# An order of their own for the first three halves of a clustered attention, with four stack copies on GpSimd and the loads re-ordered

## The chip, the core and the metric

One core of one Trainium2 chip runs the whole program in one launch: clustered attention, then two mixture-of-experts-like layers. The metric is the device time of an execution in microseconds (us). The kernel before takes 1053.87 us, the median of three runs (1053.55 to 1054.81). The engines are PE (TensorE: matmuls; its weight loads are shown apart as PEld), DVE (VectorE), ACT (ScalarE), POOL (GpSimd) and SP (SyncE, which here issues every DMA). Each engine works through its own list of instructions in the order in which the kernel wrote them, and waits at an instruction until what that one needs is there. All matmuls here have fp32 operands or fp32r (fp32 with the value rounded for TensorE's one-pass format).

## What is computed

The inputs are q, k, v of 2 batches x 8 heads x 768 rows x 64, and 16 centroids per head.

```python
q_assign = argmax(q_n @ c_n.T, -1)          # q_n, k_n, c_n: rows of unit length
k_assign = argmax(k_n @ c_n.T, -1)
scores = q @ k.T / 8
scores = where(q_assign[:, None] == k_assign[None, :], scores, -1e9)
x = softmax(scores) @ v                     # 1536 tokens x 512 after the heads are put side by side
g = elu(x @ w_in); x = g @ w_out            # 512 -> 2048 -> 512
p = probs / probs.sum(-1)                   # 4 experts, all of them used
out = sum_e p[:, e] * (relu(x @ w1[e]) @ w2[e])
```

## The kernel before

Attention goes through 8 pairs of heads (pair 0 is batch 0, heads 0 and 1). For each pair q and k are loaded, transposed by PE (tile `qkps`, line 199), and split into a high part that is exact in fp32r (`qh`, `kh`, ACT, line 201) and the rest (`ql`, `kl`, DVE, line 203). PE multiplies them with the centroids (`lps`, lines 239 and 240), ACT and DVE add the parts of that (`ltmp` line 243, `L` line 245), and the argmax over 16 centroids is a reduce, a subtract, a compare with a ramp (which breaks ties), a second reduce and an equality (lines 267 to 276: `mx`, `L`, `rk`, `mx`, `oh`). PE transposes the one-hot rows (`ohps`), and they become 16 more rows of the operands of the scores, so that the mask is part of the matmul: for the first pair in `first_onehot` (lines 304 and 306), later in `prep_onehot`.

The operands of one head's scores are four tiles, its *stacks*: QA (high q twice), KA (high k, low k), QB (one-hot rows, low q) and KB (one-hot rows, high k). The parts are 64 rows by 768, and `prep_stacks` (line 228) moves each of them from `qh`, `ql`, `kh`, `kl` with a DMA of 192 KB, six for a head. The next pair's `qh` and `kh` go to the same buffers, so they wait until those DMAs have read them.

The scores are taken in *units* of 128 query rows x 768 keys, numbered u0, u1, ... from the start (6 units to a head). Two units make a *half*, numbered w0, w1, ...; six halves make a pair. A half goes through these steps, and the letters are those of the table `AT` in the code: S scores (PE, lines 364 and 367, two buffers in PSUM), M the negated maximum of a row (DVE, line 373), E exponential and row sum (ACT, line 382), G and R the reciprocal of the sums of both units (lines 390, 394), P the scaling (POOL, line 400), T 12 transposes in three groups of four (PE, line 412, three buffers that they share with `qkps`, `lps` and `ohps`), C and L the split of a group into `ph` and `pl` (ACT line 425 and DVE line 433; for some groups ACT copies to `raw`, line 422, and POOL does both parts, lines 430 and 431), V 12 matmuls with v (PE, line 441), and X, Y, Z the sum of the two parts (ACT line 453, DVE line 461, POOL). Q are pieces of the next pairs' preparation, W pieces of the weights of the layers behind.

The order is a list: each step of each half has a time, `AT` plus 4.6 for every half plus a few shifts, and all are sorted by it and written out in that order, so each engine's list follows from it. What stands ahead of the list (the prologue) is written out by hand: loads, preparation of the first pair, 14 transposes of the identity that only keep PE at work (`warm`, line 508), the argmax of the first head. The second head's argmax, its one-hot rows and the next pair's q are put in ahead of three items of half w0.

The layers behind attention (lines 745 to 931) start when it ends, in a fixed order of their own.

## Time and profile before

| | us |
|---|---|
| median of three runs | 1053.87 |
| the profiled execution | 1049.63 |
| its span, from the first instruction to the last | 1047.9 |
| attention, about | 0 to 268 |
| PE busy, share of the span | 98% |
| DVE, ACT, POOL busy, share of the span | 70%, 50%, 37% |

The shares mix two stages: behind attention PE works almost alone, and in attention four engines are near their limit together. What the change does lies in the first 45 us, so the shares of that stretch are the ones to read. The first unit's scores start at 17.6 us, and the first exponential at 21.5 us. The page names 67.5 MB of DMA; the mean busy share of the DMA engines is 0.8 and 0.7 in the first two of its 40 slices.

### The profile page before, as it was taken

What the parts mean: (1) busy time and instruction counts of PE and PEld (TensorE: products, weight loads), DVE (VectorE), ACT (ScalarE), POOL (GpSimd) and SP (SyncE); (2) the same over time, 40 slices, a digit from 0 to 9 for tenths busy, and PEclk for the clock granted to TensorE, in tenths of its full rate; (3) what the DMA queues carried; (4) which work ended last, traced back from release to release, by engine and by line L of the source; (5) the groups of instructions that cost most, each with busy time, mean ns of one, the idle gap of its engine ahead of it and who ended that gap; (6) DMA issues with size and microseconds to landing.
All of it is one profiled execution on the core that took longest, in us unless ns stands there. A gap on an engine that the chain in (4) does not pass through costs nothing.

```text
span 1047.9 us, 16446 instructions
## 1 busy us (share of the span) xinstructions
PE 1029.1 (98%) x6253; PEld 918.4 (88%) x6253; DVE 735.4 (70%) x1248; ACT 524.2 (50%) x1081; POOL 392.8 (37%) x394
## 2 busy tenths in 40 slices
PE   8999999999999999999999999999999999999998
PEld 7989999989877888888888898999999898989897
DVE  6999989998689674326576765666666767666665
ACT  4989999988676563324442332233332333332331
POOL 2888888889578766344641000000000000000000
PEclk8999999999999999999999999999999999999999
DMA  8746664431323221010002101111101111001003
GB/s 184 186 109 155 144 145 104 111 92 33 114 96 122 81 96 66 1 41 0 1 1 81 41 1 41 41 41 41 35 7 41 41 42 41 17 25 41 1 1 121
DMA packets 61790, 67.53 MB, mean 64 GB/s; under 512 B 29008, under 2 KB 47440, under 8 KB 61712
## 3 DMA queue, kind: packets, MB, share of 16 engines
q1 hardware_dynamic: 61712, 66.49, 22.4%
q8 instruction: 49, 0.80, 0.3%
q14 instruction: 29, 0.24, 0.1%
HBM read 43.08 MB, written 3.15 MB: 44 GB/s over the span
## 4 chain that ended last, share of the span: by engine, by line
PE 84%; DVE 8%; ACT 4%; issue 2%; DMA 1%; SPq 1%; POOL 1%; DVEq 0%; ACTq 0%; POOLq 0%
PE a L915 35%; PE h L765 23%; PE h L745 10%; PE x L441 5%; PE tps L412 4%; PE s L364 2%; PE s L367 2%; DVE pl L433 2%; DVE nm L373 1%; PE lps L239 1%; PE lps L240 1%; DVE wa L710 1%; ACT ph L425 1%; PE qkps L199 1%; ACT e L382 1%
## 5 line engine op out<-in xcount | busy, mean ns | idle before, releaser
L765 PEld LDWEIGHTS h<-x,w1op 128*128 128x128 f32 x2016 | 257.4, 190 | 10.3 <-ACT r L776 1.2
L765 PE MATMUL h<-x,w1op 128*128 128x256 f32 x2016 | 261.2, 285 | 1.0 <-ACT r L776 1.0
L915 PE MATMUL a<-w2op,gh 128*128 128x512 f32 x768 | 238.4, 392 | 0.0
L915 PEld LDWEIGHTS a<-w2op,gh 128*128 128x128 f32 x768 | 138.0, 188 | 23.9
L924 DVE SCALAR_TENSOR_TENSOR acc<-a,prob,acc 128x512 f32<-128x512 f32 x180 | 129.7, 746 | 40.2 <-PE a L915 40.2
L915 PE MATMUL a<-w2op,gl 128*128 128x512 f32 x384 | 149.8, 390 | 0.0
L745 PE MATMUL h<-xT,wh 128*128 128x512 f32 x384 | 118.5, 390 | 0.6 <-DVE gg L754 0.5
L400 POOL TENSOR_SCALAR p<-e,sm 128x768 f32<-128x768 f32 x96 | 88.4, 927 | 40.2 <-DVE sm L394 29.0
L754 DVE SCALAR_TENSOR_TENSOR gg<-r,h 128x512 f32<-128x512 f32 x48 | 32.9, 685 | 96.5 <-ACT r L753 75.4
L373 DVE TENSOR_REDUCE nm<-s 128x1 f32<-128x768 f32 x96 | 90.9, 947 | 2.8 <-PE s L367 2.6
L382 ACT ACTIVATE e<-s,nm 128x768 f32<-128x768 f32 x96 | 86.6, 902 | 4.5 <-POOL p L400 2.8
L412 PE MATMUL tps<-ident,p 128*128 128x128 f32 x576 | 83.5, 277 | 2.9 <-DVE pl L433 2.7
L745 PEld LDWEIGHTS h<-xT,wh 128*128 128x128 f32 x384 | 71.9, 188 | 16.2 <-DVE gg L754 1.4
L776 ACT ACTIVATE r<-h 128x256 f32<-128x256 f32 x48 | 18.4, 384 | 134.8 <-PE h L765 134.8
L915 PEld LDWEIGHTS a<-w2op,gl 128*128 128x128 f32 x384 | 72.1, 188 | 15.6
L433 DVE TENSOR_TENSOR pl<-tps,ph 128x512 fp32r<-128x512 f32 x112 | 76.2, 683 | 6.6 <-ACT ph L425 5.2
L441 PE MATMUL x<-ph,v 128*128 128x256 f32 x288 | 76.6, 298 | 1.4 <-DVE xs L461 1.3
L752 ACT ACTIVATE r<-h 128x512 f32<-128x512 f32 x48 | 28.6, 595 | 97.7 <-PE h L745 96.9
L915 PE MATMUL a<-gh,wh 128*128 128x512 f32 x192 | 74.9, 390 | 1.0 <-ACT acc L931 0.9
L755 POOL TENSOR_SCALAR gh<-gg 128x512 fp32r<-128x512 f32 x48 | 41.0, 854 | 92.0 <-DVE gg L754 89.2
L915 PE MATMUL a<-gl,wh 128*128 128x512 f32 x192 | 74.8, 390 | 0.0
L915 PE MATMUL a<-gh,wl 128*128 128x512 f32 x192 | 74.7, 389 | 0.0
(152 smaller groups left out, 1942.1 us busy)
## 6 DMA issues: line engine op xcount, KB each, us to landing
st<-in_moe_w_dram SPq DMA_DIRECT2D x32, 512.0 KB, 4.3
st<-in_moe_w_in_dram SPq DMA_DIRECT2D x14, 512.0 KB, 3.7
st<-in_moe_w_out_dram SPq DMA_DIRECT2D x14, 512.0 KB, 4.6
QA<-qh SPq DMA_DIRECT2D x32, 192.0 KB, 4.2
nq<-in_q_dram SPq DMA_DIRECT2D x16, 192.0 KB, 3.8
nk<-in_k_dram SPq DMA_DIRECT2D x16, 192.0 KB, 3.9
nv<-in_v_dram SPq DMA_DIRECT2D x8, 384.0 KB, 3.9
QB<-ql SPq DMA_DIRECT2D x16, 192.0 KB, 4.2
```

Of the source, the lines that this page charges most:

```text
L373: dve.tensor_reduce(out=m_t[w][:, i:i + 1], in_=s_t[HALF * w + i][:, :, 0:384], axis=AX.XY, op=ALU.max, negate=True)
L382: act.activation(out=e, in_=s_t.pop(u)[:, :, 0:384], func=AF.Exp, bias=m_t[w][:, i:i + 1], accum_out=e_t[w][0][:, i:i + 1])
L400: pool.tensor_scalar(p, e_t[w][1 + i].rearrange("p a b -> p (a b)"), e_t[w][0][:, i:i + 1], 1.0, ALU.mult, ALU.mult)
L412: pe.transpose(ps[:, x, :], p_t[w][i][:, c * 128:(c + 1) * 128], ident)
L433: dve.tensor_tensor(out=l, in0=ps, in1=h.bitcast(F32), op=ALU.subtract)
L441: pe.matmul(x_t[w], lhsT=v2[j][:, r, c, :], rhs=t[:, :, c, :], start=(c == 0 and t is ph[w]), stop=(c == T - 1 and t is pl[w]),)
L745: pe.matmul(ps, lhsT=w[:, 0, f], rhs=x, start=(kk == 0 and i == 0), stop=(kk == KD - 1 and i == 2))
L754: dve.scalar_tensor_tensor(out=gg, in0=r, scalar=-1.0, in1=ps, op0=ALU.add, op1=ALU.max)
L755: pool.tensor_scalar(gh, gg, 1.0, 0.0, ALU.mult, ALU.add)
L765: pe.matmul(ps, lhsT=w[wz][kk], rhs=x[xz][:, kk], start=(start and kk + i == 0), stop=(stop and kk == 1 and i == 2), skip_group_check=True,)
L915: pe.matmul(ps, lhsT=x, rhs=y, start=(opens and i == 0), stop=(closes and i == len(ops) - 1))
L924: dve.scalar_tensor_tensor(out=t, in0=ps, scalar=pr, in1=t, op0=ALU.mult, op1=ALU.add)
```

## The change

The prologue and the first three halves are written in another order, and some of the work goes to another engine:

- `prep_stacks` for the first pair lets POOL copy one part of each of q and k for both heads (four of twelve); eight stay DMAs.
- The loads of the next pair's q and k are issued in another order with the second head's stacks (q, then the stacks, then k), and v of the first pair is loaded last. The first split of v on POOL (`prep_v`) goes from the prologue into the list, behind P of half w0.
- The argmax of q is done for both heads at once (`ramp` is twice as long), between the centroid products of k; its one-hot rows are moved out by ACT alone, a whole head at a time (before by ACT and DVE, half a head each). The argmax of k comes head by head.
- S is cut in two: the two matmuls with QA and KA (`do_SA`) are written ahead of the one-hot rows of k for u0 and u1, those with QB and KB (`do_SB`) behind them.
- The transposes of the identity are 3, 4, 5, 4 and 4, at five places, in a buffer of another pool.
- Halves w0, w1 and w2 get times of their own (`place`: 1.5 + 0.6 of `AT`, 4.6 + 0.8, 9.2 + 0.9), the Q items of w0 and w1 others, and the second head's argmax of k, the next pair's q and the split of v get fixed times (`start`).

```diff
-    ramp = const.tile([128, 1, C], F32, name="ramp")
+    ramp = const.tile([128, 1, 2 * C], F32, name="ramp")
...
-            for dst, src in parts:
-                sp.dma_start(out=dst.bitcast(F32), in_=src[rows])
+            for i, (dst, src) in enumerate(parts):
+                if j == 0 and i == r:
+
+                    pool.tensor_scalar(dst, src[rows], 1.0, 0.0, ALU.mult, ALU.add)
+                else:
+                    sp.dma_start(out=dst.bitcast(F32), in_=src[rows])
...
+            if nm == "q":
+                ps = ps_t.tile([C, S], BF16, tag="t", name="ohps")
+                for t in range(T):
+                    pe.transpose(ps[:, t * 128:(t + 1) * 128], oh[:, t, r], identb)
+                act.activation(out=dst[0:C], in_=ps, func=AF.Copy)
+                return
...
-        load(0, "v")
...
-        for nm in "qk":
-            load(1, nm)
+        load(1, "q")
         for nm in "qk":
             prep_stacks(0, nm, 1)
-        run(*(prep_logits(0, "k", i) for i in range(2)))
-        warm(14)
-        run(*(prep_argmax(0, i, g, g + 1) for i in range(3) for g in (0, 2)))
+        load(1, "k")
+        load(0, "v")
+        run(prep_argmax(0, 0, 0, 2))
+        run(prep_logits(0, "k", 0))
+        run(prep_argmax(0, 1, 0, 2), prep_argmax(0, 2, 0, 2))
+        run(prep_logits(0, "k", 1))
+        warm(3)
+        for r in range(2):
+            first_onehot(r, "q")
+        run(*(prep_argmax(0, i, 2, 3) for i in range(3)))
+        for i in range(2):
+            do_SA(0, i)
+        warm(4)
+        run(prep_argmax(0, 0, 3, 4))
         first_onehot(0, "k")
-        first_onehot(0, "q")
-        run(prep_v(0, 0))
+        warm(5)
...
-            (at + PERIOD * w + SHIFT.get((nm, w % (2 * NH)), 0) + (4 if nm[0] == "Q" and w == 0 else 0), w, nm)
...
+        def place(at, w, nm):
+            if w > 2 or nm[0] in "QW":
+                return at + PERIOD * w + ((5.5, 2.5)[w] if w < 2 and nm[0] == "Q" else 0)
+            at0, pace = ((1.5, 0.6), (4.6, 0.8), (9.2, 0.9))[w]
+            return at0 + pace * at
...
+        def start(w, i):
+            if i == 0:
+                run(*(prep_argmax(0, x, 3, 4) for x in (1, 2)))
                 first_onehot(1, "k")
                 oh_t.pop(0)
-            if w == 0 and nm == "Q0":
-                run(*(prep_qk(1, "q", i) for i in range(2)))
-                prep_stacks(1, "q", 0)
+            elif i < 3:
+                run(prep_qk(1, "q", i - 1))
+                if i == 2:
+                    prep_stacks(1, "q", 0)
+                    run(prep_v(0, 0))
+            else:
+                warm(WARM[i - 3][1])
+
+        items += [(at, 0, f"_{i}") for i, at in enumerate((3.9, 5.0, 6.5))]
+        items += [(at, 0, f"_{i + 3}") for i, (at, _) in enumerate(WARM)]
```

The same lists, as the two programs have them. First ACT from the first exponential to the fourth, before: `e_416`, `e_450`, `e_499` and `e_518` are the exponentials of u0 to u3, `qh_419` and `kh_439` the next pair's q and k, `lps` its centroid products.

```order
L382 ACTIVATE e_416,sm_415<-s_383,nm_388 128x768
L201 ACTIVATE qh_419<-qkps_421 128x384
L201 ACTIVATE qh_419<-qkps_427 128x384
L382 ACTIVATE e_450,sm_415<-s_390,nm_388 128x768
L201 ACTIVATE kh_439<-qkps_441 128x384
L201 ACTIVATE kh_439<-qkps_455 128x384
L390 ACTIVATE sm_415<-sm_415 128x2
L243 ACTIVATE ltmp_496<-lps_462 128x96
L382 ACTIVATE e_499,sm_498<-s_445,nm_452 128x768
L243 ACTIVATE ltmp_501<-lps_479 128x96
L382 ACTIVATE e_518,sm_498<-s_470,nm_452 128x768
```

And ACT after, over the same four exponentials (`e_391`, `e_412`, `e_482`, `e_519`); `ph_489<-tps_491` is C of the first group of half w0.

```order
L412 ACTIVATE e_391,sm_390<-s_355,nm_386 128x768
L323 ACTIVATE KB1_138<-ohps_402 16x384
L412 ACTIVATE e_412,sm_390<-s_358,nm_386 128x768
L420 ACTIVATE sm_390<-sm_390 128x2
L203 ACTIVATE qh_427<-qkps_429 128x384
L203 ACTIVATE kh_448<-qkps_450 128x384
L203 ACTIVATE qh_427<-qkps_455 128x384
L412 ACTIVATE e_482,sm_481<-s_414,nm_419 128x768
L455 ACTIVATE ph_489<-tps_491 128x512
L203 ACTIVATE kh_448<-qkps_484 128x384
L412 ACTIVATE e_519,sm_481<-s_438,nm_419 128x768
```

The second head's one-hot rows of k have come between the first two exponentials, and C of half w0 and the last piece of the next pair's k between the third and the fourth. On PE, the scores of u2 to u4 and the transposes of the next pair, before (`s_445` is u2):

```order
L199 MATMUL qkps_421<-ident_60,nq_290 128x128 x3
L199 MATMUL qkps_427<-ident_60,nq_290 128x128 x3
L199 MATMUL qkps_441<-ident_60,nk_293 128x128 x3
L364 MATMUL s_445<-KA0_131,QA0_128 128x384 x2
L367 MATMUL s_445<-KB0_137,QB0_134 128x384 x2
L199 MATMUL qkps_455<-ident_60,nk_293 128x128 x3
```

After, `s_414`, `s_438` and `s_467` are u2, u3 and u4:

```order
L389 MATMUL s_414<-KA0_131,QA0_128 128x384 x2
L398 MATMUL s_414<-KB0_137,QB0_134 128x384 x2
L538 MATMUL warm_421<-ident_60 128x128 x4
L201 MATMUL qkps_429<-ident_60,nq_288 128x128 x3
L389 MATMUL s_438<-KA0_131,QA0_128 128x384 x2
L398 MATMUL s_438<-KB0_137,QB0_134 128x384 x2
L201 MATMUL qkps_450<-ident_60,nk_297 128x128 x3
L201 MATMUL qkps_455<-ident_60,nq_288 128x128 x3
L389 MATMUL s_467<-KA0_131,QA0_128 128x384 x2
L398 MATMUL s_467<-KB0_137,QB0_134 128x384 x2
```

Three of the four groups of transposes have moved behind the scores of u2, two of them behind those of u3, and the fourth behind those of u4. On DVE, from the next pair's q and k to the first R of half w1 (`sm_498`), before:

```order
L203 SCALAR_TENSOR_TENSOR kl_440<-qkps_441,kh_439 128x384
L203 SCALAR_TENSOR_TENSOR kl_440<-qkps_455,kh_439 128x384
L394 RECIPROCAL sm_415<-sm_415 128x2
L245 TENSOR_TENSOR L_461<-lps_462,ltmp_496 128x3x32
L373 TENSOR_REDUCE nm_452<-s_470 128x1
L245 TENSOR_TENSOR L_461<-lps_479,ltmp_501 128x3x32
L373 TENSOR_REDUCE nm_506<-s_489 128x1
L245 TENSOR_TENSOR L_461<-lps_511,ltmp_520 128x3x32
L394 RECIPROCAL sm_498<-sm_498 128x2
```

After (`sm_481` is half w1's, `nm_526<-s_467` is M of u4):

```order
L205 SCALAR_TENSOR_TENSOR kl_449<-qkps_450,kh_448 128x384
L403 TENSOR_REDUCE nm_419<-s_438 128x1
L205 SCALAR_TENSOR_TENSOR kl_449<-qkps_484,kh_448 128x384
L463 TENSOR_TENSOR pl_490<-tps_491,ph_489 128x512
L403 TENSOR_REDUCE nm_526<-s_467 128x1
L424 RECIPROCAL sm_481<-sm_481 128x2
```

M of u4 and R of half w1 now stand behind the second piece of `kl` and behind L of the first group of half w0.

## Rows read from the trace of the kernel before

**Rows 1.** Busy time by stretch (count), granted PE clock, DMA share, GB/s
```profile
13.00:17.60 4.60, 4.60 (x27) 3.92 (x26) 2.82 (x12) 1.06 (x3) 0.00 (x0) 0.50 1.01 214
26.00:35.00 9.00, 8.38 (x62) 8.01 (x63) 8.16 (x18) 8.13 (x22) 7.97 (x10) 1.00 1.02 243
35.00:60.00 25.00, 24.03 (x186) 22.67 (x184) 24.06 (x41) 22.64 (x53) 18.90 (x22) 1.00 0.63 150
260.00:1048.00 788.00, 780.14 (x4388) 684.01 (x4386) 501.85 (x799) 302.43 (x568) 182.34 (x136) 1.00 0.13 45
```

**Rows 2.** Timeline (start, us, engine, line; idle before and releaser): next pair's k
```profile
24.92 0.87 ACT L201 ACTIVATE kh<-qkps 128x384 fp32r<-128x384 f32 x2 [0.68 <-DMA KB<-kh]
```

**Rows 3.** Timeline of the prologue
```profile
9.79 0.87 ACT L201 ACTIVATE kh<-qkps 128x384 fp32r<-128x384 f32 x2
...
11.25 0.25 DVE L245 TENSOR_TENSOR L<-lps,ltmp 128x96 f32<-128x96 f32 x1
...
12.92 3.25 PE L508 MATMUL warm<-ident 128*128 128x128 f32 x14
...
14.49 0.25 DVE L271 SCALAR_TENSOR_TENSOR rk<-L,ramp 128x96 f32<-128x96 f32 x1
14.77 0.26 DVE L274 TENSOR_REDUCE mx<-rk 128x6 f32<-128x96 f32 x1
...
16.10 1.60 PE L301 MATMUL ohps<-identb,oh 128*16 128x128 bf16 x12
...
17.02 0.55 DVE L306 TENSOR_SCALAR KB<-ohps 16x384 fp32r<-16x384 bf16 x1 [1.21 <-PE ohps L301]
...
17.63 0.97 PE L364 MATMUL s<-KA,QA 128*128 128x384 f32 x2
...
20.35 0.95 DVE L373 TENSOR_REDUCE nm<-s 128x1 f32<-128x768 f32 x1
```

**Rows 4.** Timeline of DVE and POOL, both at work on SBUF
```profile
37.53 1.28 POOL L431 TENSOR_TENSOR pl<-raw,ph 128x512 fp32r<-128x512 f32 x1
...
38.06 1.18 DVE L276 TENSOR_TENSOR oh<-rk,mx 128x384 bf16<-128x384 f32 x1
```

**Rows 5.** Timeline from u2's exponential to the first C
```profile
25.90 0.91 ACT L382 ACTIVATE e<-s,nm 128x768 f32<-128x768 f32 x1
...
26.96 0.61 PE L364 MATMUL s<-KA,QA 128*128 128x384 f32 x2
...
28.36 0.66 PE L412 MATMUL tps<-ident,p 128*128 128x128 f32 x4
...
29.05 0.60 ACT L425 ACTIVATE ph<-tps 128x512 fp32r<-128x512 f32 x1 [0.16 <-PE tps L412]
```

**Rows 6.** Groups by form, first 60 us: xcount, busy us, mean ns, idle before
```profile
L400 POOL TENSOR_SCALAR p<-e,sm 128x768 f32<-128x768 f32 x14 | 13.0, 941 | 20.5 <-DVE sm L394 19.7 <-PE qkps L199 0.8
...
L433 DVE TENSOR_TENSOR pl<-tps,ph 128x512 fp32r<-128x512 f32 x14 | 9.6, 684 | 1.0 <-ACT ph L425 0.7 <-issue 0.2
...
L431 POOL TENSOR_TENSOR pl<-raw,ph 128x512 fp32r<-128x512 f32 x4 | 5.1, 1284 | 0.3
...
L203 DVE SCALAR_TENSOR_TENSOR kl<-qkps,kh 128x384 fp32r<-128x384 f32 x6 | 3.1, 552 | 0.8 <-ACT kh L201 0.7
...
L430 POOL TENSOR_SCALAR ph<-raw 128x512 fp32r<-128x512 f32 x4 | 2.5, 620 | 0.2 <-ACT raw L422 0.2
```

**Rows 7.** The chain that ended last, where PE runs without a gap
```profile
46.26 0.35 PE s L367 x2
46.62 0.33 PE qkps L199 x3
46.95 0.71 PE x L441 x6
47.66 0.44 PE tps L412 x4
```

**Rows 8.** Timeline: the first matmul with v (half w0)
```profile
34.46 0.36 PE L441 MATMUL x<-ph,v 128*128 128x256 f32 x1
```

More of the change, by code (lines that the diff above doesn't have):

```diff
@@ L36 @@
 POOL_SPLITS = (2, 4, 6, 11)
+WARM = ((2.65, 4), (4.8, 4))
 BIG = float(2.0 ** 100)
@@ L262, in prep_argmax @@
                 L, mx, rk, oh = (x.rearrange("p t g c -> p (t g) c") for x in (L_t[j], *oh_t[j]))
-            else:
-                L, mx, rk, oh = (x[:, :, g0] for x in (L_t[j], *oh_t[j]))
-            top = mx.to_broadcast([128, T * n, C])
+            elif n == 1:
+                L, mx, rk, oh = (x[:, :, g0] for x in (L_t[j], *oh_t[j]))
+            else:
+                L, mx, rk, oh = (x[:, :, g0:g1] for x in (L_t[j], *oh_t[j]))
+            shape = [128, T, n, C] if 1 < n < 4 else [128, T * n, C]
+            top = mx.to_broadcast(shape)
             if part == 0:
@@ L270, in prep_argmax @@
             elif part == 1:
+                both = len(shape) == 4
+                x, y = (z.rearrange("p t g c -> p t (g c)") if both else z for z in (L, rk))
+                order = ramp if both else ramp[..., 0:C]
                 dve.scalar_tensor_tensor(
-                    out=rk, in0=L, scalar=0.0, in1=ramp.to_broadcast([128, T * n, C]), op0=ALU.is_ge, op1=ALU.mult
+                    out=y, in0=x, scalar=0.0, in1=order.to_broadcast([128, x.shape[1], order.shape[2]]),
+                    op0=ALU.is_ge, op1=ALU.mult,
                 )
@@ L300, in first_onehot @@
                 for t in range(3):
-                    pe.transpose(ps[:, t * 128:(t + 1) * 128], oh[:, 3 * i + t, r + 2 * (nm == "k")], identb)
+                    pe.transpose(ps[:, t * 128:(t + 1) * 128], oh[:, 3 * i + t, r + 2], identb)
                 o = dst[0:C, i * 384:(i + 1) * 384]
@@ L356, in do_S, with do_SA @@
         def do_S(w, i):
+            do_SA(w, i)
+            do_SB(w, i)
+        def do_SA(w, i):
             u = HALF * w + i
+            if u in s_t:
+                return
             j, r, t = u // UP, (u % UP) // T, u % T
             s = (2 * j + r) % NSET
-            ps = ps_s.tile([128, 2, 512], F32, tag="s", name="s")
+            ps = s_t[u] = ps_s.tile([128, 2, 512], F32, tag="s", name="s")
             c = slice(t * 128, (t + 1) * 128)
@@ L364, in do_S, with do_SB @@
                 pe.matmul(ps[:, n, 0:384], lhsT=QA[s][:, c], rhs=KA[s][:, m], start=True, stop=False)
+        def do_SB(w, i):
+            u = HALF * w + i
+            j, r, t = u // UP, (u % UP) // T, u % T
+            s = (2 * j + r) % NSET
+            c = slice(t * 128, (t + 1) * 128)
             for n in range(2):
                 m = slice(384 * n, 384 * n + 384)
-                pe.matmul(ps[:, n, 0:384], lhsT=QB[s][:, c], rhs=KB[s][:, m], start=False, stop=True)
-            s_t[u] = ps
+                pe.matmul(s_t[u][:, n, 0:384], lhsT=QB[s][:, c], rhs=KB[s][:, m], start=False, stop=True)
         def do_M(w, i):
@@ L504, in warm @@
         def warm(n):
-            ps = ps_t.tile([128, 3, 128], F32, tag="t", name="warm")
+            ps = ps_x.tile([128, 2, 128], F32, tag="x", name="warm")
             for i in range(n):
-                pe.transpose(ps[:, i % 3, :], ident, ident)
+                pe.transpose(ps[:, i % 2, :], ident, ident)
         c0, cn = load_centroids()
@@ L516, in attention @@
         for c in range(C):
-            dve.memset(ramp[..., c:c + 1], float(C - c))
+            dve.memset(ramp[..., c::C], float(C - c))
         for i in range(NSET):
@@ L547, in attention @@
                   Z=do_XS, Q=do_Q, W=do_W)
-        items = sorted(
-            (at + PERIOD * w + SHIFT.get((nm, w % (2 * NH)), 0) + (4 if nm[0] == "Q" and w == 0 else 0), w, nm)
-            for nm, at in AT.items() for w in range(NW)
-        )
-        for at, w, nm in items:
-            if w == 0 and nm == "S0":
-                run(*(prep_argmax(0, i, g, g + 1) for i in range(3) for g in (1, 3)))
-            if w == 0 and nm == "E0":
-                first_onehot(1, "q")
+        def place(at, w, nm):
[3 more added lines that the diff above has]
+            return at0 + pace * at
+        items = [
+            (place(at, w, nm) + SHIFT.get((nm, w % (2 * NH)), 0), w, nm) for nm, at in AT.items() for w in range(NW)
+        ]
+        def start(w, i):
+            if i == 0:
+                run(*(prep_argmax(0, x, 3, 4) for x in (1, 2)))
                 first_onehot(1, "k")
                 oh_t.pop(0)
-            if w == 0 and nm == "Q0":
-                run(*(prep_qk(1, "q", i) for i in range(2)))
-                prep_stacks(1, "q", 0)
+            elif i < 3:
[7 more added lines that the diff above has]
+        items += [(at, 0, f"_{i + 3}") for i, (at, _) in enumerate(WARM)]
+        do["_"] = start
+        for at, w, nm in sorted(items):
             do[nm[0]](w, int(nm[1:]))
```

## The prediction, made before the changed kernel ran

> **What bounds the kernel now.** I read the busy time by stretch first. Behind attention PE is busy for 780.14 of 788 us and the others far less: whatever delays the end of attention is handed through to the end. In attention there is no single bound: from 35 to 60 us PE is busy 24.03 of 25 us, DVE 24.06, ACT 22.64 [rows 1]. So the kernel's time is a start-up, and then a dense stretch of fixed work. The question for a change in the first 40 us is at what time the engines have done a given amount of that work. PE is the measure, since it is bound in both stages.
>
> The chain of waits and the timeline come next. The chain runs back to the issue of the next pair's loads and of the second head's stacks: the next pair's `kh` waits until a stack's DMA has read the buffer. But the wait itself is 0.68 us of ACT [rows 2], and the DMA engines' share is 1.02 from 26 to 35 us without holding up anything else that I found [rows 1]. So the chain's long DMA piece is worth 0.7 us, not its length.
>
> **The change part by part: transfers.** Four of twelve stack parts of 192 KB go, and the second head's stacks are issued ahead of k of the next pair. That takes away the 0.68 us of [rows 2] at most. POOL pays four copies of 64 x 768; the nearest row is P with 128 x 768, 0.94 us [rows 6], so between half of that and 0.94 each; I take 0.94. POOL has nothing else to do there. v now lands behind k of the next pair; its split on POOL stands behind P of w0 (27 us or later), so I cost this at nothing: the cover is more than the length of a transfer, and if it were gone the wait would fall on V of w0.
>
> **The prologue.** Up to the first half of q's centroid sums nothing moves. From the second half's sum (11.25) the argmax of q for both heads runs alone on DVE: sum 0.28, then five dependent steps, with one sum for k between them (0.18). A dependent step of 96 elements takes 0.28 (14.49 to 14.77); a reduce of 768 takes 0.95 and one of 96 takes 0.26, so about 0.10 more for 192 [rows 3], and 0.38 a step. 11.25 + 0.28 + 0.18 + 5 x 0.38 = 13.6 for q's one-hot rows. Here the copies cost something. The equality of DVE (two inputs from SBUF) starts at 38.06 under a POOL operation that ends at 38.81, and lasts 1.18, to 39.24: it ran 0.43 behind POOL's end [rows 4]. In the changed prologue POOL's copies of `kh`, `qh` and `kl` stand back to back from 10.66, when `kh` is whole [rows 3]: to 11.6, 12.6, and the third behind the subtract. The subtract of DVE, ready at 11.9, is held to 12.6 (0.7), the compare to the end of the third copy (another 0.4 to 0.7). That is +1.1: 14.7.
>
> The Trainium skill (SBUF — State Buffer, section Who interferes with whom) says that a VectorE operation with two SBUF inputs and a GpSimd one that reads SBUF exclude each other for a whole instruction. The rows [rows 4] agree to 0.43 us. By it the copies delay q's argmax as just worked out; if the engines merely shared, the 13.6 would hold.
>
> Then PE, whose clock was granted at 0.50 of full, that is 1.2 GHz, from 13.0 to 17.6 [rows 1] in spite of 14 transposes of the identity there: 12 one-hot transposes 1.6; the four products with KA of u0 and u1 1.5 (two took 0.97 with the way in); four identity transposes 4 x 3.25/14 = 0.93; the one-hot rows of k for the first head until both engines have moved them out, 16.10 to 17.57, 1.5 [rows 3]. Sum 5.5, then the two products with KB 0.45. From 13.6 that is 19.6, from 14.7 it is 20.3 (the last pieces at the higher clock, which I take to come back at about 18.5, where the scores of u1 run at their later speed). In before the scores of u0 begin at 17.63, but their maximum at 20.35, because the second head's argmax stands ahead of it. So the start is not lost: M of u0 is 0.7 earlier or equal.
>
> **The halves.** Now the new lists, counted from the moment when u0's scores are whole (t = 0):
>
> - M of u0 and u1, 2 x 0.95 [rows 3], then three dependent steps of the second head's argmax: 2.75.
> - Three transposes and the way to ACT (half of 16.10 to 17.02) 0.45, the one-hot rows on ACT 0.5: 3.7. Only then E of u1, since ACT has these rows in front of it; 0.9: 4.6.
> - u3's scores wait for that PSUM buffer: 0.15 + 0.71, then two groups of the next pair's transposes 0.66, 0.25 to ACT, `qh` 0.49 [rows 2, 7]: 6.9. Only then E of u2.
> - u4's scores wait for E of u2, and the first transposes of w0 stand behind them. In before E of u2, scores of u4, six centroid products, four transposes, C: 25.90 to 29.05, 3.15 [rows 5]. The new list has the same and three more transposes, 0.33 [rows 7]: C at 10.4.
> - C 0.6, `kh` 0.49: 11.45. E of u3 starts here, 4.55 behind E of u2.
> - DVE has `kl` 0.55, L 0.68 and M of u4 0.95 ahead of R of w1: 13.6. P of u2 and u3 2 x 0.94, then the group that POOL splits, 0.62 + 1.28 [rows 6]: 17.5. The matmuls with v of w0 need it.
> - Six of those were waiting but for the last, four transposes 0.44, six matmuls with v 0.71, four transposes 0.44 [rows 7]: u6's scores begin at t = 19.15.
>
> So u6's scores begin at 38.75 (t = 0 at 19.6) or 39.45 (20.3). By then PE has done scores of u0 to u5, all preparation of the next pair, 12 + 8 transposes and 12 matmuls with v. In before it had, at 34.46 [rows 8], that preparation, scores of u0 to u7, 24 transposes, and none of the v matmuls: to compare, add 1.42 for v, take off 2 x 0.71 and 0.44: 34.0. **The changed kernel is 4.75 or 5.45 us late with the same work.** I take the second, by [rows 4]. Some is given back: PE idled 0.97 of 25 us from 35 to 60 [rows 1], and the work that is still missing needs no long chain, so 0.7 off. Sum +4.8.
>
> Every single wait here is one that the lists impose: an engine that waits has work further down its own list that it can't take.
>
> On the profiled execution that is 1049.63 + 4.8 = 1054.4. That execution was 4.24 below the median of the runs, so I forecast 1053.87 + 4.8 = **1058.7 us**. Its own range is 1056.3 (half of the lateness hidden behind later idle time) to 1061.7 (what follows).
>
> **Rivals.**
>
> *Absorbed.* From w3 on the order is that of before, and the changed kernel has w0 finished by then, so DVE and ACT have loose ends that it can fill; the time would be 1053.5 to 1056. For: what is missing is scores, which wait for nothing but buffers. Against: PE, DVE and ACT have only 4, 4 and 9% free [rows 1], 1 us in 25, and five are to be regained.
>
> *Faster.* The new order does what its times say: u6's scores 11 to 12 us behind those of u0, as the list has them (13.8 against 1.5 or 2.2). Then they begin at 31 to 32, and with the work done earlier PE is 2 to 3 us ahead of the 34.0: 1051 to 1052. For: M of u0 is not later, and less stands on DVE. Against: three waits above are each a PSUM buffer or a tile that the list itself puts late; to get there E of u2 and of u3 would have to start 3 us earlier than the instructions in front of them on ACT end. It decides by the time of u3's exponential: before about 27 us this rival is right.
>
> *Clock.* In the stretch from u0 to u6 PE has gaps up to 2 us, and it fell to 1.2 GHz once in before with shorter ones [rows 1]. If it falls again for 6 us, the PE pieces there take some 2 us more: 1061 to 1063.
>
> *The change buys nothing in transfers and costs nothing in order* (the four copies hide, the chain is PE's as before): a saving of the 0.68 us and the two DVE moves of one-hot rows, 0.55 each, off an engine that is near its limit: 1052 to 1053.5.
>
> **How the numbers follow.** Less than 0.2% of the time (2.1 us) I count as no change, about what a measurement of this kernel can tell. Forecast 0.60, all slower. Absorbed 0.13, of it 0.08 the same and 0.05 slower. Clock 0.06, slower. Faster 0.15, faster. Nothing gained or lost 0.06, 0.05 the same and 0.01 faster. That makes 0.71 slower, 0.13 the same, 0.16 faster. The range of 8 in 10 reaches from 1052.0 (it leaves out most of the faster rival, 0.12) to 1062.0 (it leaves out half of the clock's): the low end takes in the two that end near the time before.
>
> **What would show it.** In the profile of the changed kernel: no DMA wait of ACT at `kh`; subtract and compare of the two-head argmax each 0.5 us or more longer than their size asks for; the first maximum at 19.6 to 20.4; exponentials of u1, u2, u3 some 2.6, 5.8 and 10.4 us behind that of u0; ACT idle for 2 us or more ahead of the first C; u6's scores near 39 us; the end of attention, about 268 now, 4 to 5 us later. Wrong would be: u3's exponential at 27 us or earlier, or the second pair's start within 1 us of before in spite of a late u6 (then it was absorbed).

## The result, and the profile after

The changed kernel takes **1068.07 us** (median of 6 runs, 1065.34 to 1071.36) against 1053.89 (6 runs, 1053.50 to 1054.81): ratio 1.0137, 95% interval 1.0118 to 1.0157, 14.2 us slower. Slower was forecast, but 4.8 us of it, and the time lies outside the range. The profiled executions differ by more than the medians, 1068.09 against 1049.63 us (spans 1066.3 and 1047.9): that of before was one of its quicker ones. So what the two traces show adds up to 18.4 us, not to 14.2.

Nothing behind attention takes part: its first matmul starts at 269.48 in before and at 288.04 now, 18.56 later, and the spans differ by 18.4. Nearly all of it arises between 25 and 60 us (18.0 us at u11's scores, which start at 60.59 now). Here is that stretch in the changed kernel, by busy time of each engine and granted clock (PEclk):

```profile
core 0: us, PE busy (x) PEld busy (x) DVE busy (x) ACT busy (x) POOL busy (x), PEclk, DMA share, GB/s
20.00:25.00 5.00, 3.13 (x25) 2.71 (x25) 3.74 (x7) 2.55 (x6) 0.00 (x0) 1.00 0.46 129
25.00:30.00 5.00, 3.48 (x24) 3.21 (x23) 2.78 (x6) 2.24 (x5) 3.26 (x4) 0.93 0.45 113
30.00:35.00 5.00, 3.07 (x14) 2.27 (x12) 2.70 (x6) 2.92 (x8) 0.59 (x1) 0.50 0.97 232
35.00:40.00 5.00, 4.58 (x20) 4.59 (x20) 1.09 (x4) 1.75 (x5) 4.54 (x6) 0.50 0.21 49
40.00:45.00 5.00, 5.00 (x25) 5.00 (x25) 1.11 (x3) 1.47 (x4) 0.00 (x0) 0.50 0.79 220
45.00:50.00 5.00, 4.02 (x23) 3.54 (x22) 3.21 (x7) 2.92 (x7) 2.26 (x3) 0.87 0.80 203
50.00:55.00 5.00, 3.50 (x17) 2.85 (x16) 3.32 (x6) 2.78 (x6) 3.87 (x5) 0.82 0.01 2
55.00:60.00 5.00, 3.39 (x21) 2.89 (x20) 2.52 (x5) 2.30 (x5) 2.18 (x3) 0.84 0.00 0
```

Two things are there that before has not. From 20 to 35 us PE is idle for a third of the time. And from about 29.3 us its clock is granted at 0.50 of full, 1.2 GHz, until about 46.3, and again near 53 to 57. In the trace of before it stood at 1.00 from 20 to 60 us; its first five are

```profile
20.00:25.00 5.00, 4.12 (x34) 3.23 (x34) 4.91 (x10) 3.54 (x9) 0.00 (x0) 1.00 0.87 207
```

and [rows 1] has the rest. The changed kernel's gaps on PE in this stretch are these (start, duration, in square brackets the idle time before and what ended it):

```profile
22.87 0.50 PE L320 MATMUL ohps<-identb,oh 128*16 128x128 bf16 x6 [1.87 <-DVE oh L289]
...
27.91 0.62 PE L389 MATMUL s<-KA,QA 128*128 128x384 f32 x2 [1.51 <-ACT e L412]
...
32.76 1.97 PE L442 MATMUL tps<-ident,p 128*128 128x128 f32 x8 [1.66 <-DVE kl L205]
35.41 0.42 PE L245 MATMUL lps<-cc,qh 128*128 128x64 f32 x1 [0.69 <-ACT raw L452]
```

From 35.4 on PE is without a gap to 46.3, at half speed, while DVE and ACT wait for it: its busy share looks like that of a bound engine, but it does the work of half of one.

Up to 32 us the trace goes as forecast. These are ACT's exponentials (`e`), the first way out (`ph`, that is C of w0) and `kh`:

```profile
21.23 0.90 ACT L412 ACTIVATE e<-s,nm 128x768 f32<-128x768 f32 x1 [1.99 <-DVE nm L403]
23.68 0.88 ACT L412 ACTIVATE e<-s,nm 128x768 f32<-128x768 f32 x1
26.86 0.90 ACT L412 ACTIVATE e<-s,nm 128x768 f32<-128x768 f32 x1
...
31.13 0.60 ACT L455 ACTIVATE ph<-tps 128x512 fp32r<-128x512 f32 x1 [3.28 <-PE tps L442]
31.63 0.48 ACT L203 ACTIVATE kh<-qkps 128x384 fp32r<-128x384 f32 x1
32.00 0.91 ACT L412 ACTIVATE e<-s,nm 128x768 f32<-128x768 f32 x1
```

Measured behind u0's exponential: u1 2.45, u2 5.63, u3 10.77 us (forecast 2.6, 5.8, 10.4). u3's stands behind C and `kh`, as the lists said. From then on the two part, as the starts of the scores show (us, read from PE's timelines; "fill" is the run e1 below, in which the clock stays up until 46 us):

| unit | before | changed | later by | fill | later by |
|---|---|---|---|---|---|
| u4 | 26.96 | 27.91 | 0.95 | 27.90 | 0.94 |
| u5 | 28.77 | 38.00 | 9.23 | 35.61 | 6.84 |
| u6 | 31.00 | 44.82 | 13.82 | 39.30 | 8.30 |
| u9 | 37.01 | 54.00 | 16.99 | 48.27 | 11.26 |
| u13 | 47.85 | 66.68 | 18.83 | 60.48 | 12.63 |
| u24 | 77.78 | 96.31 | 18.53 | 90.12 | 12.34 |

u6's rows, in before, in the changed kernel and in e1:

```profile
31.00 0.59 PE L364 MATMUL s<-KA,QA 128*128 128x384 f32 x2
```

```profile
44.82 0.99 PE L389 MATMUL s<-KA,QA 128*128 128x384 f32 x2
```

```profile
39.30 0.59 PE L389 MATMUL s<-KA,QA 128*128 128x384 f32 x2
```

From u13 on the difference stays within 0.3 us, over hundreds of instructions: the lists are the same there, and the engines fall into one fixed pattern that neither loses nor regains. So the lateness at u13 is the lateness at the end.

### The profile page after: what moved, and what is told of

Its sections match the earlier page's. It is cut to its first block, busy times and chain, and to the rows that moved or that the text cites. A ratio compares the mean times of both kernels' runs of the same rounds, so it can differ in the third digit from the quotient of the medians.

```text
span 1066.3 us, 16443 instructions
## 1 busy us (share of the span) xinstructions
PE 1038.6 (97%) x6259; PEld 926.3 (87%) x6259; DVE 735.1 (69%) x1241; ACT 525.6 (49%) x1081; POOL 396.1 (37%) x398
## 4 chain that ended last, share of the span: by engine, by line
PE 85%; DVE 7%; ACT 4%; issue 2%; POOL 1%; DMA 0%; ACTq 0%; DVEq 0%; SPq 0%; POOLq 0%
PE a L966 35%; PE h L816 23%; PE h L796 10%; PE x L471 5%; PE tps L442 5%; PE s L389 3%; PE s L398 2%; DVE pl L463 1%; DVE nm L403 1%; ACT e L412 1%; POOL p L430 1%; PE lps L245 1%; PE lps L246 1%; DVE wa L761 1%; ACT ph L455 1%
## 5 line engine op out<-in xcount | busy, mean ns | idle before, releaser
L442 PE MATMUL tps<-ident,p 128*128 128x128 f32 x576 | 86.6, 283 | 6.1 <-DVE pl L463 2.6
L827 ACT ACTIVATE r<-h 128x256 f32<-128x256 f32 x48 | 18.4, 384 | 134.8 <-PE h L816 134.8
L442 PEld LDWEIGHTS tps<-ident,p 128*128 128x128 f32 x576 | 66.9, 144 | 11.4 <-DVE pl L463 4.4
L471 PE MATMUL x<-pl,v 128*128 128x256 f32 x288 | 73.7, 287 | 1.2 <-POOL pl L461 1.1
```

The source lines that it names most:

```text
L442: pe.transpose(ps[:, x, :], p_t[w][i][:, c * 128:(c + 1) * 128], ident)
L471: pe.matmul(x_t[w], lhsT=v2[j][:, r, c, :], rhs=t[:, :, c, :], start=(c == 0 and t is ph[w]), stop=(c == T - 1 and t is pl[w]),)
```

## The experiments

Traces of single executions differ in when the first fall of the clock ends (near 19 us in the changed kernel, e1 and e5, near 21 in e6, e8 and e9). In those three it falls a second time from about 24 to 28 us, and u4 comes 2.5 to 2.9 us later. So mechanisms are read from traces below, and prices from medians. All runs are compared with runs of the kernel before on the same chip (medians 1053.7 to 1054.2).

### Clock or order

**e1_fill.** `WARM` holds pairs of time and count of transposes of the identity in the list:

```diff
-WARM = ((2.65, 4), (4.8, 4))
+WARM = ((2.65, 4), (4.8, 4), (6.6, 13), (8.05, 16), (8.45, 12))
```

> The changed kernel with 41 more transposes of the identity on PE in the three gaps of 26 to 35.4 us (13 ahead of u4's scores, 16 behind the first group of w0's transposes, 12 behind the third); they compute nothing. Theory A (two costs: the lists make the start 4.8 us late as forecast, and the gaps then drop PE's clock from 29.3 to 46 us, which costs the other 9): the granted clock stays at 1.0 from 20 to 46 us and the time is 1058 to 1060 us. Rival B (the lists alone cost it all, the clock falls beside them): the clock stays up, the time is 1064 us or more. If the clock falls all the same the run tells nothing: 1066 to 1070 us.

1062.91 us (1061.89 to 1064.52), ratio 1.0097 (1.0081 to 1.0113): 5.2 us less than the changed kernel by the medians, won by work that computes nothing. The time lies between the two theories. The clock stayed up where the gaps were filled, and fell once more behind a gap that was not:

```profile
25.00:30.00 5.00, 4.90 (x40) 4.63 (x39) 2.77 (x6) 2.25 (x5) 3.27 (x4) 1.00 0.44 111
30.00:35.00 5.00, 5.00 (x46) 4.67 (x44) 2.84 (x6) 3.30 (x8) 1.40 (x2) 1.00 1.00 238
35.00:40.00 5.00, 5.00 (x41) 5.00 (x41) 1.96 (x5) 2.96 (x8) 3.74 (x5) 1.00 0.22 50
40.00:45.00 5.00, 3.83 (x23) 2.81 (x21) 4.23 (x7) 3.82 (x9) 3.38 (x5) 1.00 0.96 258
45.00:50.00 5.00, 3.86 (x17) 3.66 (x17) 2.12 (x5) 1.68 (x5) 3.88 (x4) 0.66 0.59 163
```

With the clock held, u6's scores start at 39.30; the forecast's hand tally said 39.45. So for a PE at full clock the tally had the time right, but not its last link. It let POOL's split hold the matmuls with v of w0. In e1 that split ends at 37.34, and the first of those matmuls starts before it, and PE's rows show no wait from 23 to 42 us:

```profile
36.06 1.28 POOL L461 TENSOR_TENSOR pl<-raw,ph 128x512 fp32r<-128x512 f32 x1
...
36.99 0.37 PE L471 MATMUL x<-ph,v 128*128 128x256 f32 x1
```

Here it is PE's own list from 33 us on (fillers, 18 centroid products, u5's scores, v, transposes) that takes until 39.30. That the two agree to 0.15 us is in part luck. What the tally did not have are the waits behind u6, up to 54 us:

```profile
42.38 0.62 PE L389 MATMUL s<-KA,QA 128*128 128x384 f32 x2 [0.81 <-ACT e L412]
44.23 0.44 PE L442 MATMUL tps<-ident,p 128*128 128x128 f32 x2 [0.22 <-POOL p L430]
46.34 0.57 PE L471 MATMUL x<-pl,v 128*128 128x256 f32 x1 [1.14 <-POOL pl L461]
52.44 0.52 PE L295 MATMUL ohps<-identb,oh 128*64 128x128 bf16 x6 [0.78 <-DVE pl L463]
53.86 0.63 PE L442 MATMUL tps<-ident,p 128*128 128x128 f32 x4 [0.90 <-DVE ql L205]
```

That is 3.85 us of PE's idle time, each a wait of the same kind as those before u6: the next thing in PE's list is not ready. The trace of before has 0.97 us of such waits from u6 to u13.

**e5_fill2** and **e9_fill3** add fillers to `WARM`: `(18.39, 6), (19.5, 14)`, and then `(23.35, 8), (24.21, 9)`.

> The kernel with transposes of the identity in three gaps (e1), and 20 more of them, ahead of u8's scores (6) and ahead of the first matmuls with v of w1 (14), where the clock still fell at 46.2 us; they compute nothing. Theory A2 (what the lists cost by waits alone is about 10 us, and every fall of the clock comes on top): the clock stays at 1.0 from 20 to 60 us, the scores from u13 on stand about 10 us behind before instead of 12.4, the time is 1059.5 to 1061.5 us. Rival (that fall was covered by waits for POOL): the clock holds and the time stays at 1062 to 1064 us.

> The kernel of e5 with 17 more transposes of the identity in the two gaps of 50 to 52.5 us (8 ahead of the next pair's one-hot transposes, 9 ahead of w3's first transposes), so that all gaps from 26 to 53 us are filled; they compute nothing. Theory A3 (the lists cost 10.4 us by their waits, the value at u10 and u11 in e5, and the fall at 53.5 us in e5 took back what holding the clock before had won): the clock stays at 1.0 from 20 to 60 us, u13's scores 10.2 to 10.8 us behind before, 1060 to 1061.5 us. Rival (the schedule into which the halves lock is 12.4 us late whatever the clock does): the clock holds, u13 stays 12.0 us or more behind, 1062 to 1063.5 us.

1062.80 us (ratio 1.0087, 1.0066 to 1.0108) and 1063.14 (1.0084, 1.0066 to 1.0102): no time is won over e1. These are the rivals' times, but not for the rivals' reason. In e5's trace the clock holds to 53 us, and u10 and u11 stand 10.4 us behind before; then a fall near 53.5 takes it to 12.3 at u12. In e9's it stays up from 28 us on, but it had fallen a second time from 24.5 to 27.9:

```profile
25.00:30.00 5.00, 5.00 (x30) 4.87 (x30) 2.08 (x5) 2.67 (x8) 0.78 (x1) 0.71 0.01 2
```

With that, and with its early fall ending later, u4 began 3.8 us late. From u4 to u13 it loses 10.2 us with the clock up. So the waits of the lists cost about 10 us in both traces. The 8 us that remain of the changed kernel's 18.4 would then be clock; that is a subtraction, and what filling wins in the medians is 5.2. The traces also suggest why the further fillers win nothing: each of the three has one more fall of 3.4 us, in e1 from 46.4, in e5 from 53.6, in e9 from 24.5, and 12 of the 14 filled runs have the same mean granted clock, 0.995. The one at 0.997, the value of most quick runs of before (1049.2 to 1051.0), is the fastest: 1061.14. That is 10 to 12 us above those runs, which agrees with the price of the lists, and 6.9 below the changed kernel's median.

### Which part of the change

**e2_oldlist** keeps the prologue, the copies and the loads of the change, and gives all halves their times of before (it also leaves out the 8 identity transposes in the list):

```diff
-            if w > 2 or nm[0] in "QW":
-                return at + PERIOD * w + ((5.5, 2.5)[w] if w < 2 and nm[0] == "Q" else 0)
-            at0, pace = ((1.5, 0.6), (4.6, 0.8), (9.2, 0.9))[w]
-            return at0 + pace * at
+            return at + PERIOD * w + (4 if nm[0] == "Q" and w == 0 else 0)
...
-        items += [(at, 0, f"_{i}") for i, at in enumerate((3.9, 5.0, 6.5))]
+        items += [(at, 0, f"_{i}") for i, at in enumerate((1.74, 4.34, 4.35, 7.2))]
```

> The changed kernel with the list times of before for all halves (and no transposes of the identity in the list); prologue, copies on POOL and order of loads stay changed. Theory A (the lists are the cause of all of it): u0's maximum at 20.3 us as in the changed kernel, exponentials of u1 and u2 within 5 us of u0's, no fall of the clock behind 20 us, and the time of before: 1052.5 to 1055 us. Rival C (prologue, copies and loads have a large part): 1058 us or more.

1052.23 us (1051.58 to 1054.54), ratio 0.9995 (0.9984 to 1.0007): the time of before. The lists, with those 8 transposes, are the whole loss.

**e3_newlist** is the reverse: prologue and transfers of before, `place` and `start` of the change.

> The kernel before with the new times for the first three halves and the transposes of the identity in that list; prologue, stacks and loads are those of before, both heads' argmax stands ahead of the first scores' maximum. Theory A: u3's exponential 10 us or more behind that of u0, a second fall of the clock behind 26 us, and 1062 to 1069 us. Rival C: within 2 us of before, 1052 to 1056 us.

1065.91 us, ratio 1.0134 (1.0106 to 1.0161), with the clock at 0.50 from 22.3 to 25.7 and from 32.6 to 42.8 us. u3's exponential came 11.2 us behind u0's (20.54 and 31.69). Theory A had all three.

**e15_qnew** and **e16_qold** cut the list change in two. e15 is e2 with the next pair's preparation at its new times (`Q` 5.5 and 2.5 later, its q at 5.0 and 6.5); e16 is the changed kernel with that preparation at its old times (4 later for w0, its q at 4.34 and 4.35).

> The kernel with the changed prologue and the old times of all halves (e2), but the next pair's preparation at the new, later times (Q items of w0 and w1 1.5 and 2.5 later, its q in two pieces at 5.0 and 6.5). Theory L (the pace of the halves causes the waits): 1052 to 1056 us. Rival Q (the late preparation causes them: the next pair's one-hot and centroid products then stand in front of scores): 1060 us or more.

> The changed kernel with the next pair's preparation at its old times (its q ahead of u2's scores, its Q items 1.5 and 2.5 earlier); the halves w0 to w2 keep the new times. Theory L: 1062 us or more. Rival Q: 1053 to 1058 us. Half and half: 1058 to 1062 us.

1061.39 us (ratio 1.0071, 1.0045 to 1.0096) and 1063.83 (1.0102, 1.0080 to 1.0123). Against before on the same chip (1053.9) that is 7.5 and 9.9 us of the 14.2: each half of the list change alone costs half of it or more, and they do not add up. Either opens gaps on PE (1.34 and 1.46 us for an exponential in e15's trace, 0.7 to 1.1 us for POOL, an exponential, DVE's split and `ql` in e16's), and in either the clock falls: 0.50 from about 25 to 45 us in e15, for 3.4 us each from 24.4, 38.0 and 55.0 in e16. e15 has the time of rival Q and e16 that of theory L, so neither part alone is the cause. How much of each is clock was not measured.

**e8_w0old** and **e6_w0late** try the link that the forecast named. e8 gives w0 its old times (`w == 0 or w > 2` in `place`); e6 moves T, C, L, V, X, Y and Z of w0 later by 2.0.

> The changed kernel with w0 at its old times (and the split of v behind P of w0 as before the change of lists); w1 and w2 keep the new ones, as does the preparation of the next pair. Theory A2: u3's exponential has neither C of w0 nor kh in front of it and starts at 28 to 29 us, no fall of the clock between 20 and 40 us, and 1054 to 1060 us. Rival (the pace of w1 and w2 or the later preparation of the next pair costs as much): 1062 us or more.

> The changed kernel with w0's transposes, their way out, its matmuls with v and what follows them 2.0 later in the list, so that u3's exponential stands ahead of the first way out (C) on ACT. Theory A2 (the forecast's link: u3's exponential behind C of w0 is what holds u5 and all that follows): u3's exponential at 28 to 29 us instead of 32.0, u5's scores at 29 to 33 us instead of 38, and 1056 to 1062 us. Rival (the link is one of several alike, the next takes its place): u6's scores still at 42 us or later, 1065 us or more.

1067.99 us (ratio 1.0129, 1.0104 to 1.0154) and 1062.93 (1.0088, 1.0065 to 1.0111). In e8 the pace of w1 and w2 and the late preparation are enough for the whole loss, the rival's time, though u3's exponential stands only 3.4 us behind u2's there. e6 lies between its two expectations. u3's exponential starts ahead of C, 3.42 us behind u2's (33.09 and 29.67) instead of 5.14, in an execution that is 2.8 us later at u4. But PE then waits for `L` at two groups of transposes (0.34 and 1.12 us), the clock is at 0.50 from 34.6 to 44.9, and u6's scores start at 43.03 instead of 44.82. The medians give 5.1 us back, as much as the fillers. So that link is worth part of the loss, and others alike remain.

**e4_alldma** makes all stack parts DMAs again (the branch with `pool.tensor_scalar` in `prep_stacks` is gone).

> The changed kernel with all twelve first stack parts as DMAs, no copy on POOL. Theory A: subtract and compare of the two-head argmax return to 0.4 us or less each, q's one-hot rows and u0's maximum come 0.7 to 1.1 us earlier, and the rest follows shifted, with the same fall of the clock: 1066 to 1068 us. A rival (the copies' hold on DVE is what opens the gaps): the clock does not fall behind 20 us, under 1062 us. A rival on the other side (four more transfers in the queue come late and hold u2 to u4): 1070 us or more.

1070.31 us (1069.00 to 1073.03), ratio 1.0170 (1.0148 to 1.0191): if anything slower. That is the time of the rival on the other side, but little of its mechanism shows: no row of PE waits for a DMA from 20 to 60 us, ACT has one such wait (1.74 us, at the next pair's first `qh`), and u3 and u4 come 1.2 and 1.3 us later behind a fall of the clock from 22.8 to 26.2. The run also prices the copies' hold on DVE. In the changed kernel the copies and the two-input steps of the argmax lie like this (POOL, then DVE):

```profile
11.65 0.83 POOL L232 TENSOR_SCALAR QA<-qh 64x768 fp32r<-64x768 f32 x1
12.56 0.83 POOL L232 TENSOR_SCALAR KA<-kl 64x768 fp32r<-64x768 f32 x1
...
11.92 0.76 DVE L278 TENSOR_TENSOR L<-L,mx 128x192 f32<-128x192 f32 x1
...
12.78 0.82 DVE L283 SCALAR_TENSOR_TENSOR rk<-L,ramp 128x192 f32<-128x192 f32 x1
```

and without the copies:

```profile
11.96 0.36 DVE L275 TENSOR_TENSOR L<-L,mx 128x192 f32<-128x192 f32 x1
...
12.40 0.35 DVE L280 SCALAR_TENSOR_TENSOR rk<-L,ramp 128x192 f32<-128x192 f32 x1
```

Subtract and compare last 0.40 and 0.47 longer under a copy, and each ends 0.2 behind the copy's end; q's one-hot rows come at 14.02 instead of 13.17 in the trace without. The rule of the Trainium skill (SBUF — State Buffer, section Who interferes with whom), an exclusive hold between a VectorE instruction with two SBUF inputs and a GpSimd one that reads SBUF, agrees with these rows to 0.2 us. It decides little here: u0's maximum is 0.26 earlier without the copies.

### Can an idle PE be afforded?

**e7_late0** moves the rest of the second head's argmax and its one-hot rows in e2 from 1.74 to 6.0. **e10_old176** moves them to 1.76, which exchanges two instructions of ACT and nothing else. **e12_old176fill** is e10 with `WARM = ((1.755, 12), (15.01, 6))`.

> The changed prologue with the old list times (e2), and in it the rest of the second head's argmax of k and its one-hot rows at 6.0 instead of 1.74; u6 is the first unit that needs them. Theory: in e2 u0's exponential stood behind one-hot rows on ACT, at 22.8, though its maximum was there at 21.2; now it starts at 21.3, u1's at 22.3 or earlier, and what is 1.0 to 1.9 us earlier there stays so: 1050.3 to 1051.5 us. Rival (the time is set later, by the schedule into which the halves lock): 1052 to 1054 us, as e2.

> The kernel with the old list times (e2) and two instructions of ACT exchanged: u0's exponential ahead of the one-hot rows of k for the second head. Theory: u0's exponential at 21.3 instead of 22.8, u2's scores no later, 0 to 1.5 us earlier from there on: 1051 to 1052.3 us. Rival (the one-hot rows come later and hold u1's maximum or the transposes of the next q through their PSUM buffer): 1053 us or more.

> The kernel of e10 with 18 transposes of the identity on PE: 12 in the gap of 20.6 to 22.0 us, 6 in that of 32.4 to 33.1; they compute nothing. Theory (runs of e2 at 1053.6 to 1054.5 are those in which the clock fell a second time): all runs within 1 us of the fastest, 1050.5 to 1052 us. Rival (the gaps are too short to matter): the same time as e10 within 0.5 us, with the same spread.

1055.81 us (1.0026, 1.0012 to 1.0040), 1052.61 (1.0004, 0.9990 to 1.0018) and 1052.63 (0.9991, 0.9981 to 1.0001). e7 was expected faster and is 3.6 us slower than e2: u0's and u1's exponentials did come earlier (22.23 and 23.86, in an execution whose scores start 0.64 later), but PE, with less to do ahead of u2's scores, waited 1.80 us for the next pair's k, and its clock stood at 0.50 from 24.0 to 27.5 and from 30.9 to 41.1 us. e10's exchange is worth nothing: its time lies between the two expectations. e12's theory missed. All its runs have a mean granted clock of 0.996 or 0.997, where five of e10's twelve have 0.995, and in the traces a fall from 24.1 to 27.5 is in e10 and not in e12. So the fillers held the clock; but the median is the same and the spread little smaller (1051.60 to 1053.90 against 1051.18 to 1054.43). Holding the clock is not always worth the time that holds it.

### What the kernel before itself loses

**e11_beforefill** is the kernel before with `warm(6)` ahead of the second head's one-hot rows and `warm(4)` ahead of u7's scores.

> The kernel before with 10 transposes of the identity: 6 ahead of the second head's one-hot transposes (the gaps of 19 to 22 us), 4 ahead of u7's scores (32.4 us); they compute nothing. Theory (the kernel before also loses some 3 us of clock in most of its runs, since its times lie at 1050.4 or at 1053.6 us): most runs at 1050 to 1051 us. Rival (the two times have another cause): a median of 1053.5 to 1054.5 us, or later by what the transposes delay.

1053.84 us (1049.48 to 1055.67), ratio 0.9988 (0.9975 to 1.0002): no gain (five of 12 runs at 1049.5 to 1050.5, where before has seven of 29 at 1049.2 to 1050.4). But its profiled execution was one of the later ones, and shows what the trace of before does not:

```profile
20.00:25.00 5.00, 3.06 (x24) 2.28 (x21) 3.63 (x7) 3.40 (x8) 0.00 (x0) 1.00 0.73 173
25.00:30.00 5.00, 5.00 (x25) 4.84 (x25) 3.65 (x8) 3.12 (x9) 3.04 (x4) 0.60 0.99 212
30.00:35.00 5.00, 5.00 (x23) 5.00 (x24) 2.48 (x6) 2.37 (x7) 1.73 (x3) 0.50 1.10 248
```

Its chain of waits names a stack's DMA that held the next pair's q (start and duration), and PE's row the gap that came of it:

```profile
17.82 5.78 DMA QB<-ql
```

```profile
24.34 0.55 PE L199 MATMUL qkps<-ident,nk 128*128 128x128 f32 x3 [1.32 <-DVE ql L203]
```

A fall of the clock from 26.0 to 36.2 us behind a gap of 1.32 us. The same queue ran faster in the trace of before: there the second part of QA took 4.7 us to land, here 5.8, and `qh` starts behind it, after 1.47 us without work on ACT. The kernel before has two groups of times, and the clock tells them apart: of its 103 runs beside the experiments, the 24 at 1049.2 to 1051.0 us have a mean granted clock of 0.996 to 1.000, and the 79 at 1052.5 to 1056.7 one of 0.992 to 0.995. So most of its runs have more low clock than its own trace [rows 1], which is of the quicker group. That this has the cause seen in e11 is likely, but not shown: no run of before itself in the later group was traced.

**e13_transfers**, **e14_loads**, **e17_qstacks**, **e18_qstackspool** are the kernel before with parts of the change's transfers. e14: q of the next pair, second head's stacks, k, and v last, its split behind P of w0. e13: the same with the four POOL copies. e17 only moves the stacks of q between the loads of q and k; e18 is e17 with the four copies:

```diff
         for nm in "qk":
             load(1, nm)
-        for nm in "qk":
             prep_stacks(0, nm, 1)
...
-            for dst, src in parts:
-                sp.dma_start(out=dst.bitcast(F32), in_=src[rows])
+            for i, (dst, src) in enumerate(parts):
+                if j == 0 and i == r:
+                    pool.tensor_scalar(dst, src[rows], 1.0, 0.0, ALU.mult, ALU.add)
+                else:
+                    sp.dma_start(out=dst.bitcast(F32), in_=src[rows])
```

> The kernel before with the transfer part of the change alone: four stack parts copied by POOL, the second head's stacks issued ahead of k of the next pair, v last and its split behind P of w0; prologue and lists as before. Theory T (in most executions of the kernel before a stack's DMA holds the next pair's qh, PE then idles for 1.3 us and its clock falls from 26 to 36 us, some 3 us): no wait for a DMA at qh or kh, no fall of the clock behind 20 us, most runs at 1049 to 1051 us. Rival (the copies on POOL hold DVE's argmax of the first head, as in the changed prologue, and the later start eats it): 1053 us or more.

> The kernel before with the order of the loads alone (second head's stacks ahead of k of the next pair, v last, its split behind P of w0); all stack parts are DMAs. Theory T: most of the gain of e13, most runs at 1049 to 1051 us. Rival (the stacks' DMAs come as late by their number alone): the two groups of times of before, median 1053 to 1054.5 us.

> The kernel before with one exchange in the DMA queue: the second head's stacks of q are issued between the loads of the next pair's q and k instead of behind both. Theory T2 (the queue's order decides: qh must be free before 22 us and the next pair's k there by 23 us; here both hold): no PE gap over 1 us between 18 and 26 us, no fall of the clock behind 20 us in most runs, median 1049.5 to 1051.5 us. Rival (k comes some 1.9 us later and PE waits for it as in e14): 1054 us or more.

> The kernel of e17 with four of the first pair's stack parts copied by POOL, as in the change. Theory T2: the queue is shorter by two parts ahead of k and one more behind it, so k lands earlier than in e17: median 1049.5 to 1051.5 us, and fewer runs above 1053 us than e17. Rival (POOL's copies hold DVE in the prologue and shift the clock's first fall): 1052 to 1055 us, in two groups as e13.

| run | median | range | ratio (interval) | PE's wait for k in its trace |
|---|---|---|---|---|
| e14 | 1059.38 | 1058.11 to 1060.61 | 1.0066 (1.0047 to 1.0085) | 3.31 |
| e17 | 1057.31 | 1050.07 to 1058.75 | 1.0023 (1.0002 to 1.0043) | 2.06 |
| e13 | 1054.62 | 1050.80 to 1057.28 | 1.0010 (0.9990 to 1.0030) | 1.46, no fall behind it |
| e18 | **1049.77** | 1048.82 to 1052.92 | **0.9971 (0.9956 to 0.9986)** | 0.41 |

e13, e14 and e17 missed their expectation. With stacks as DMAs ahead of it k lands too late in e14 and e17, and the gap is merely another. e13 has two groups, six runs at 1050.8 to 1052.7 and six at 1056.6 to 1057.3; its trace is of the first, and what holds the second was not traced. This is e17's row, and e18's:

```profile
23.79 0.52 PE L199 MATMUL qkps<-ident,nk 128*128 128x128 f32 x3 [2.06 <-DMA nk<-in_k_dram]
```

```profile
23.72 0.52 PE L199 MATMUL qkps<-ident,nk 128*128 128x128 f32 x3 [0.41 <-DMA nk<-in_k_dram]
```

```profile
20.00:25.00 5.00, 4.29 (x32) 3.29 (x30) 4.55 (x12) 3.41 (x9) 0.00 (x0) 0.86 0.61 118
25.00:30.00 5.00, 5.00 (x39) 4.72 (x37) 4.50 (x11) 4.23 (x14) 2.88 (x4) 1.00 0.94 204
30.00:35.00 5.00, 4.53 (x36) 4.22 (x35) 4.80 (x9) 4.71 (x12) 4.73 (x6) 1.00 1.10 245
```

e18 beats both kernels: q's buffers are free, k is there, PE has 4.29 of 5 us to do, and the clock stays at 1.00 behind the first fall, which ends at 21.4. It is 0.3% faster than before, with 10 of 12 runs under 1051 us. Its trace is no faster than the quick one of before (spans 1048.4 and 1047.9): what it wins is to be nearly always in the quick group. It takes from the change the copies on POOL and one step in the queue. The copies alone, with the queue as before, were not run.

## Why the prediction was wrong

- **The start, right.** No DMA wait at `kh`; the argmax held by the copies, by 0.87 in the sum of its two steps where 1.1 was said; u0's maximum at 20.24 where 19.6 to 20.4 was said.
- **The chain of lists up to u6, right at full clock.** Exponentials within 0.4 us of the tally, u6's scores at 39.30 (e1) for 39.45, the last link by luck: PE's own work, not POOL's split, ends there. By e2 the lists are also the whole loss. The "absorbed" and "faster" rivals are out: u3's exponential came at 32.0, not before 27.
- **"Some is given back", wrong in sign.** The step put 0.7 us off, since what was missing "needs no long chain". This step failed. From u6 on PE waited for an exponential, for P and the split on POOL, for the split on DVE and for `ql`, 3.85 us in e1 up to 54 us. In the traces with the clock up the lists cost about 10 us, not 4.8.
- **The clock, left out of the sum.** This step failed too. It was a rival with 0.06, for 6 us of low clock, a length given without a reason, and 2 us of time. Measured: 17 us at 1.2 GHz and a second fall of 3.4 us, about 8 us of the 18.4 between the traces by subtraction, 6.9 by the one filled run at 0.997; 5.2 us of the medians come back by fillers. The price for one us of low clock was not far off (2 for 6, against 8 for 20.4); the length was. It was set by what came behind the gaps: at half speed PE itself became the bound, with a backlog of scores, centroid products and transposes in front of it, and the clock did not come back when the gaps ended (35.4) but 11 us later.
- **The base.** The sum was made on a quick execution of before and added to the median. By the mean clocks the 4.2 us between the two are not noise: the median run has low clock that the traced one lacks, and e11 shows where it may lie. Whether the changed kernel pays that as well, in another place, is not shown.
- **The transfers, undervalued.** "That takes away the 0.68 us of [rows 2] at most": that was the wait in one trace. In e11's the same queue costs a gap and a fall of the clock, and e18 shows 4.0 us between the medians.

## What to carry to other kernels

Price a gap on PE not by its length but by what its clock does afterwards: here gaps of 1.3 to 3.3 us were followed by 3 to 20 us at half speed, and 41 fillers that compute nothing, or one exchange in a DMA queue with four copies on POOL, were worth 4 to 5 us. But fillers can also only move the fall (e5, e9) or cost what they win (e12). Where times of one kernel fall into two groups, profile until there is a trace of each, before taking a sum from either. When an order by times is squeezed, look at the whole stretch until the lists are the same again; here nothing was given back behind it.

## What the runs showed of the hardware that was not expected

- The granted clock fell while PE was in work again, not in the gap: in the changed kernel PE waited 1.51 us until 27.91, worked from there on, and fell at about 29.3; in e11 it waited 1.32 until 24.34 and fell at 26.0; in e7 1.80 until 24.01, and it fell 0.05 us later. It then stayed at 0.50 through more than 10 us without a gap (35.4 to 46.3; in e14 from 26.2 to 39.9, PE busy throughout).
- Not every gap does it, and the same gap does not always. e2's trace has a wait of 1.45 us ahead of 22.01, e13's one of 1.46 ahead of 23.58 (in a run of its quicker half), and both stay at 1.00 from 20 us on; e10 has the wait of 1.45 too, and falls. The wait of 1.87 us ahead of the second head's one-hot transposes has no fall behind it before the next gap in the changed kernel, e1 and e5, and one of 3.4 us in e6, e8, e9 and e16, all executions in which the early fall ended later. e9's row, with the fall at 24.5:

```profile
24.16 0.55 PE L320 MATMUL ohps<-identb,oh 128*16 128x128 bf16 x6 [1.87 <-DVE oh L289]
```

- Executions of one program fall into groups 3 to 4 us apart (1049.7 and 1053.8), and their mean granted clock differs with them (0.996 to 1.000 and 0.992 to 0.995).
